# Windowed attention in 256-token units on 64-wide TensorE tiles, issued in a planned order, with the first 128 tokens of the dense expert taken as the stationary operand

## The chip, the cores and the metric

The kernel runs on one core of a Trainium2 chip. The metric is the device time of one execution in microseconds. Before the change it is 609.06 us, the median of three runs (608.77 to 610.55).

Engine names are those of the profile: PE is TensorE, PEld its weight loads, DVE is VectorE, ACT ScalarE, POOL GpSimd, and SP the engine whose queue issues the DMAs.

## The reference

Three layers follow one another, on 1152 tokens (2 sequences of 576) of width 512:

```python
def _attn_ref(q, k, v):                      # (2, 8, 576, 64) each
    scores = scale * np.matmul(q, k.transpose(0, 1, 3, 2))
    mask = (rel >= 0) & (rel < 64)           # rel = query position - key position
    scores = np.where(mask, scores, -1000000000.0)
    attn = softmax(scores)                   # with + 1e-09 in the denominator
    return np.matmul(attn, v)

def _moe_ref(x, domain_probs, w1, w2):       # 4 experts, all of them for every token
    for e in range(E):
        h = np.maximum(x @ w1[e], 0.0)       # 512 -> 1024
        out += p[:, e:e + 1] * (h @ w2[e])   # 1024 -> 512

def _moe2_ref(x, modality_id, w_gate, modality_bias, w1, w2):
    # 8 experts; each token goes through the one that its gate picks
```

## The kernel before, in words

Everything is kept in fp32 precision. The dense products split each operand into a high and a low part of a faster format (xh and xl, wh and wl, hh and hl) and add three products, high x high, high x low and low x high. The attention products run on plain fp32 operands, each of which the chip executes as two passes of a matmul.

**Attention.** A query block of 64 tokens sees its own 64 keys and the 64 before. The kernel works in units of two or three blocks (`units`), one pair of heads at a time: 7 units x 4 head pairs = 28 steps. A step n goes through stages, each a small function: `at_T` transposes q and k (PE), `at_Q` copies k out (ACT) and writes q into a block-diagonal tile `qbd`, so that one 128x128 matmul serves both heads (DVE), `at_K` brings the last 64 keys of the unit before (POOL), `at_S` multiplies to scores on PE, adds the mask and takes the row maxima (DVE), `at_E` takes the exponential with its row sums (ACT), `at_N` makes reciprocals (DVE) and scales (POOL), `at_X` transposes the weights (PE, copy on ACT), `at_O` multiplies by v (PE) and copies the high part (ACT), `at_L` writes the low part xl (DVE). `attn_half` issues one half step, in a software pipeline of five steps: each call holds stages of several steps.

**Expert 0.** Its tokens are taken in groups of 256, 256, 256 and 384. `moe1_group` does the first product in eight parts f of 12 matmuls (`mm1_at`, L346), with the weights stationary and the tokens moving, and then the second product, one 128-token tile at a time, in four parts of six matmuls (`mm2_part`, L372), and `add_x2` writes the result into acc (L382). After each part a hook runs; `hook_e0` lets it issue a quota of attention half steps, so that attention stands between the dense matmuls. Before the first group, 13 attention steps are issued with dummy matmuls (`warm`, L82) between them, and the first three parts f of the first group are fed one slice at a time (`early`).

**Order.** Every engine takes its instructions in the order in which the program issues them. Before, that order is the order of the calls. Behind expert 0 the experts 1 to 3, the gate and the eight routed experts follow; the change does not touch them.

Of the kernel before, what the change touches and what calls it, by code (L numbers as in the profile page):

```python
# [5 lines left out]
F32 = mybir.dt.float32  # L6
# [9 lines left out]
def build(tc, q, k, v, probs, w1, w2, mid, wg, mbias, m2w1, m2w2, out):  # L16
    nc = tc.nc
# [7 lines left out]
    U = 192  # L25
    NU = NT // U
    UPB = S // U
# [3 lines left out]
    with ctx:  # L31
# [10 lines left out]
        pa = ctx.enter_context(tc.tile_pool(name="pa", bufs=1, space=PSUM))  # L42

        ident = const.tile([128, 128], F32, name="ident")
        mask0 = const.tile([128, 3, 128], F32, name="mask0")
        mask1 = const.tile([128, 3, 128], F32, name="mask1")
# [6 lines left out]
        qbd = [const.tile([128, 3, 128], F32, name=f"qbd{i}") for i in range(3)]  # L53

        with tc.manual_schedule():
# [4 lines left out]
            for t in qbd:  # L60
                nc.vector.memset(t, 0.0)

            nc.vector.memset(ident4, 0.0)
            for i in range(4):
                nc.gpsimd.affine_select(out=ident4, in_=ident4, compare_op=ALU.not_equal, fill=1.0,
                                        base=-32 * i, pattern=[[-1, 32]], channel_multiplier=1)
            nc.gpsimd.memset(mask1, 0.0)
            for hh in range(2):
                m = mask1[hh * 64:(hh + 1) * 64]

                nc.gpsimd.affine_select(out=m, in_=m, compare_op=ALU.is_ge, fill=-1.0e9,
                                        base=-1, pattern=[[0, 3], [1, 128]], channel_multiplier=-1)
                nc.gpsimd.affine_select(out=m, in_=m, compare_op=ALU.is_ge, fill=-1.0e9,
                                        base=64, pattern=[[0, 3], [-1, 128]], channel_multiplier=1)
            nc.gpsimd.tensor_copy(out=mask0, in_=mask1)
            nc.gpsimd.memset(mask0[:, 0, 0:64], -1.0e9)

            def warm(n):

                ps = pm.tile([128, 512], F32, tag="mm", name="psW")  # L80
                for _ in range(n):
                    nc.tensor.matmul(out=ps[:, 0:128], lhsT=ident, rhs=ident, start=True, stop=True)  # L82

            qu, ku, vu = {}, {}, {}
# [5 lines left out]
            def load_unit(u, heads=((0, H),)):  # L90
                b, t, nb = units[u]
                if u not in qu:
                    for dst, nm in ((qu, "qu"), (ku, "ku")):
                        dst[u] = at.tile([96, 2, H, D], F32, tag=nm, name=nm)
                n = 32 * nb
                for h0, h1 in heads:
                    for src, dst in ((q, qu), (k, ku)):
                        for r in range(2):
                            nc.sync.dma_start(
                                out=dst[u][0:n, r, h0:h1, :],  # L100
                                in_=src[b, h0:h1, 64 * t:64 * (t + nb), :].rearrange("h (p r) d -> r p h d", r=2)[r])

            def load_v(i):
                b, j = divmod(i, S // 64)
                x = at.tile([128, H * D], F32, tag="vu", name="vu", bufs=6)
                if j == 0:
                    nc.gpsimd.memset(x[0:64], 0.0)
                    nc.sync.dma_start(out=x[64:128].rearrange("p (h d) -> p h d", d=D),
                                      in_=v[b, :, 0:64, :].rearrange("h p d -> p h d"))
                else:  # L110
                    nc.sync.dma_start(out=x.rearrange("p (h d) -> p h d", d=D),
                                      in_=v[b, :, 64 * j - 64:64 * j + 64, :].rearrange("h p d -> p h d"))
                vu[i] = x
# [25 lines left out]
            def load_half(c, half):  # L139
                o = slice(512 * half, 512 * (half + 1))  # L140
                nc.sync.dma_start(out=raw[0, c][:, o], in_=w1[0, 128 * c:128 * (c + 1), o])

# [20 lines left out]
            def split_hi(c, half):  # L163
                key = 0
                if half == 0:
                    wh[c] = wp.tile([128, 1024], F32R, tag=f"wh{c}", name=f"wh{c}")
                    wl[c] = wp.tile([128, 1024], F32R, tag=f"wl{c}", name=f"wl{c}")
                o = slice(512 * half, 512 * (half + 1))
                nc.scalar.activation(out=wh[c][:, o], in_=raw[key, c][:, o], func=ACTF.Copy)

            def split_lo(c, half):
                o = slice(512 * half, 512 * (half + 1))
                eng = nc.gpsimd if c == 2 or (half == 1 and c == 0) else nc.vector
                eng.tensor_tensor(out=wl[c][:, o], in0=raw[0, c][:, o], in1=wh[c][:, o].bitcast(F32), op=ALU.subtract)  # L174
                if half == 1:
                    raw.pop((0, c))
                    cnt["split"] += 1
                    pump()
# [8 lines left out]
            kT = {}  # L187
            kprev = {}
            Tps, Pn, PT, Ops = {}, {}, {}, {}
# [5 lines left out]

            def at_T(n):
                b, t, nb, u, hp = unit_of(n)
                m = 32 * nb
                ps = pa.tile([128, 512], F32, tag="T", name="psT")
                for src, o in ((qu[u], 0), (ku[u], 192)):  # L200
                    for r in range(2):
                        nc.tensor.transpose(out=ps[:, o + m * r:o + m * r + m],
                                            in_=src[0:m, r, 2 * hp:2 * hp + 2, :].rearrange("p h d -> p (h d)"),
                                            identity=ident[0:m, 0:m])
                Tps[n] = ps

            def at_Q(n):
                b, t, nb, u, hp = unit_of(n)
                m = 32 * nb
                ps = Tps.pop(n)  # L210
                kt = kT[n]
                nc.scalar.activation(out=kt[:, 64:64 + 2 * m].rearrange("q (m r) -> q m r", r=2),
                                     in_=ps[:, 192:192 + 2 * m].rearrange("q (r m) -> q m r", r=2), func=ACTF.Copy)
                qb = qbd[n % 3]
                for hh in range(2):
                    nc.vector.tensor_scalar(
                        out=qb[64 * hh:64 * hh + 64, 0:nb, 64 * hh:64 * hh + 64].rearrange(
                            "q i (p r) -> q i p r", r=2),
                        in0=ps[64 * hh:64 * hh + 64, 0:2 * m].rearrange("q (r i p) -> q i p r", r=2, i=nb),
                        scalar1=0.125, scalar2=None, op0=ALU.mult)  # L220

            def at_K(n):

                b, t, nb, u, hp = unit_of(n)
                kt = at.tile([128, 256], F32, tag="kT", name="kT", bufs=5)
                if t == 0:
                    nc.gpsimd.memset(kt[:, 0:64], 0.0)
                else:
                    kp, o = kprev[hp]
                    nc.gpsimd.tensor_copy(out=kt[:, 0:64], in_=kp[:, o:o + 64])  # L230
                kT[n] = kt
                kprev[hp] = (kt, 64 * nb)

            def at_S(n):
                b, t, nb, u, hp = unit_of(n)
                ps = pa.tile([128, 3, 128], F32, tag="S", name="psS")
                kt = kT.pop(n)
# [3 lines left out]
                p = at.tile([128, 3, 128], F32, tag="sm", name="sm", bufs=3)  # L241
                nc.vector.tensor_tensor(out=p[:, 0:nb], in0=ps[:, 0:nb], in1=(mask0 if t == 0 else mask1)[:, 0:nb],
                                        op=ALU.add)
                st = at.tile([128, 8], F32, tag="st", name="st", bufs=3)
                nc.vector.tensor_reduce(out=st[:, 0:nb], in_=p[:, 0:nb], axis=AX.X, op=ALU.max, negate=True)
                stat[n] = (st, p)

            def at_E(n):
                b, t, nb, u, hp = unit_of(n)
                st, p = stat[n]  # L250
                for i in range(nb):
                    nc.scalar.activation(out=p[:, i, :], in_=p[:, i, :], func=ACTF.Exp, bias=st[:, i:i + 1],  # L252
                                         accum_out=st[:, 3 + i:4 + i])
# [851 lines left out]
```

## Time and profile before

| what | before |
|---|---|
| median of 3 runs | 609.06 us (608.77 to 610.55) |
| the profiled execution's own time | 610.33 us |
| its span, first to last instruction | 608.5 us |
| PE busy | 594.0 us, 98% of the span |
| DVE busy | 268.1 us, 44% |
| ACT busy | 205.8 us, 34% |
| POOL busy | 80.8 us, 13% |

An engine's busy time counts its instructions, and matmuls overlap: a row's duration is from its start to its modelled end, while the next one has started. The time that a stream of matmuls takes is read from one start to the next. The x behind a PE row counts passes, so an fp32 matmul of the attention counts twice.

### The profile page before, as it was taken

What the parts mean: (1) busy time and instruction counts of PE and PEld (TensorE: products, weight loads), DVE (VectorE), ACT (ScalarE), POOL (GpSimd) and SP (SyncE); (2) the same over time, 40 slices, a digit from 0 to 9 for tenths busy, and PEclk for the clock granted to TensorE, in tenths of its full rate; (3) what the DMA queues carried; (4) which work ended last, traced back from release to release, by engine and by line L of the source; (5) the groups of instructions that cost most, each with busy time, mean ns of one, the idle gap of its engine ahead of it and who ended that gap; (6) DMA issues with size and microseconds to landing.
All of it is one profiled execution on the core that took longest, in us unless ns stands there. A gap on an engine that the chain in (4) does not pass through costs nothing. (4 is left out here: it accounts for less than half of the span.)

```text
span 608.5 us, 9147 instructions
## 1 busy us (share of the span) xinstructions
PE 594.0 (98%) x3518; PEld 535.8 (88%) x3518; DVE 268.1 (44%) x618; ACT 205.8 (34%) x498; POOL 80.8 (13%) x124
## 2 busy tenths in 40 slices
PE   7989999999999999999999999999999999999995
PEld 6878899999999898989898999989898989897964
DVE  3888866542444121244321242426158598233310
ACT  2788565442313020223110131303043464333420
POOL 3354311111000000000000000000001203324221
PEclk7999999999999999999999999999999999999998
DMA  5776912000134000042200022000403466426520
GB/s 130 195 168 210 236 36 52 3 1 1 68 73 127 12 1 1 0 139 69 71 1 0 1 70 69 1 0 32 160 1 139 123 226 216 155 67 217 170 87 32
DMA packets 56463, 51.10 MB, mean 84 GB/s; under 512 B 41183, under 2 KB 41183, under 8 KB 56416
## 3 DMA queue, kind: packets, MB, share of 16 engines
q1 hardware_dynamic: 54736, 45.19, 25.2%
q0 software_dynamic: 1680, 5.29, 2.5%
q8 instruction: 29, 0.48, 0.3%
q14 instruction: 18, 0.15, 0.1%
HBM read 45.71 MB, written 4.95 MB: 83 GB/s over the span
## 5 line engine op out<-in xcount | busy, mean ns | idle before, releaser
L346 PE MATMUL ps<-xh,wh 128*128 128x384 f32 (+2 forms) x544 | 176.7, 325 | 0.2 <-DVE hl L356 0.2
L346 PE MATMUL ps<-xh,wl 128*128 128x384 f32 (+2 forms) x544 | 173.3, 318 | 1.3 <-DVE wl L174 0.9
L346 PE MATMUL ps<-xl,wh 128*128 128x384 f32 (+2 forms) x544 | 173.4, 319 | 0.0
L355 ACT ACTIVATE hh<-ps 128x384 fp32r<-128x384 f32 (+2 forms) x136 | 61.9, 455 | 288.2 <-PE ps L346 283.5
L372 PE MATMUL ps<-wh,hh 128*128 128x512 f32 (+1 forms) x368 | 146.8, 399 | 0.4 <-DVE hl L356 0.4
L372 PE MATMUL ps<-wh,hl 128*128 128x512 f32 (+1 forms) x368 | 143.8, 391 | 0.0
L372 PE MATMUL ps<-wl,hh 128*128 128x512 f32 (+1 forms) x368 | 143.6, 390 | 0.0
L356 DVE SCALAR_TENSOR_TENSOR hl<-ps,hh 128x384 fp32r<-128x384 f32 (+2 forms) x136 | 69.5, 513 | 138.6 <-ACT hh L355 138.5
L346 PEld LDWEIGHTS ps<-xh,wl 128*128 128x128 f32 x544 | 102.6, 189 | 1.7 <-DVE wl L174 1.1
L346 PEld LDWEIGHTS ps<-xh,wh 128*128 128x128 f32 x544 | 102.5, 188 | 1.2 <-DVE hl L356 0.4
L346 PEld LDWEIGHTS ps<-xl,wh 128*128 128x128 f32 x544 | 102.7, 189 | 0.6
L372 PEld LDWEIGHTS ps<-wh,hh 128*128 128x128 f32 (+1 forms) x368 | 68.8, 187 | 16.0 <-issue 1.7
L372 PEld LDWEIGHTS ps<-wh,hl 128*128 128x128 f32 (+1 forms) x368 | 68.7, 187 | 15.2
L372 PEld LDWEIGHTS ps<-wl,hh 128*128 128x128 f32 (+1 forms) x368 | 68.8, 187 | 13.2
L384 DVE SCALAR_TENSOR_TENSOR acc<-ps,prob,acc 128x512 f32<-128x512 f32 x27 | 20.3, 750 | 94.6 <-PE ps L372 94.6
L160 DVE TENSOR_TENSOR wl<-raw,wh 128x1024 fp32r<-128x1024 f32 x44 | 54.8, 1259 | 9.3 <-ACT wh L156 9.3
L838 POOL DMA_INDIRECT xr<-x2d,idg x11 | 12.4, 1130 | 332.1 <-DVE ids L549 329.5
L156 ACT ACTIVATE wh<-raw 128x1024 fp32r<-128x1024 f32 x52 | 53.3, 1051 | 0.0
L262 POOL TENSOR_TENSOR sm<-sm,rs 128x384 f32<-128x384 f32 (+1 forms) x28 | 21.7, 774 | 90.6 <-DVE rs L261 72.1
L252 ACT ACTIVATE sm<-sm,st 128x128 f32<-128x128 f32 x72 | 27.9, 391 | 0.2
L160 POOL TENSOR_TENSOR wl<-raw,wh 128x1024 fp32r<-128x1024 f32 x8 | 19.3, 2413 | 33.3 <-ACT wh L156 33.2
L287 ACT ACTIVATE xh<-psO 64x192 fp32r<-64x192 f32 (+1 forms) x56 | 16.9, 301 | 19.6 <-PE psO L281 18.3
(176 smaller groups left out, 431.7 us busy)
## 6 DMA issues: line engine op xcount, KB each, us to landing
raw<-in_moe_w_dram SPq DMA_DIRECT2D x56, 512.0 KB, 3.9
vu<-in_v_dram SPq DMA_DIRECT2D x16, 256.0 KB, 3.9
x2d<-acc SPq DMA_DIRECT2D x3, 780.0 KB, 3.5
raw<-in_moe_w_dram SPq DMA_DIRECT2D x8, 256.0 KB, 4.6
acc<-in_moe_w_dram SPq DMA_DIRECT2D x4, 512.0 KB, 7.7
qu<-in_q_dram SPq DMA_DIRECT2D x8, 192.0 KB, 3.4
ku<-in_k_dram SPq DMA_DIRECT2D x8, 192.0 KB, 4.0
qu<-in_q_dram SPq DMA_DIRECT2D x4, 128.0 KB, 3.4
```

The costliest lines, as they stand in the source:

```text
L156: nc.scalar.activation(out=hi, in_=x, func=ACTF.Copy)
L160: eng.tensor_tensor(out=lo[:, o], in0=x[:, o], in1=hi[:, o].bitcast(F32), op=ALU.subtract)
L252: nc.scalar.activation(out=p[:, i, :], in_=p[:, i, :], func=ACTF.Exp, bias=st[:, i:i + 1], accum_out=st[:, 3 + i:4 + i])
L262: nc.gpsimd.tensor_tensor(out=p[:, 0:nb], in0=p[:, 0:nb], in1=rs[:, 0:nb].to_broadcast([128, nb, 128]), op=ALU.mult)
L287: nc.scalar.activation(out=oh, in_=ps[a, 0:nb, a], func=ACTF.Copy)
L346: nc.tensor.matmul(out=ps[:, 0:n], lhsT=a[kk][:, fs], rhs=b_[:, kk, gs], start=(kk == 0 and term == 0), stop=(kk == KD - 1 and term == 2))
L355: nc.scalar.activation(out=hi[:, 0:n], in_=ps[:, 0:n], func=ACTF.Relu)
L356: nc.vector.scalar_tensor_tensor(out=lo[:, 0:n], in0=ps[:, 0:n], scalar=0.0, in1=hi[:, 0:n].bitcast(F32), op0=ALU.max, op1=ALU.subtract)
L372: nc.tensor.matmul(out=ps[0:m], lhsT=a[f][:, ts_], rhs=b_[c][:, o:o + 512], start=(f == 0 and a is hh_t and b_ is wh), stop=(f == KF - 1 a ...
L384: nc.vector.scalar_tensor_tensor(out=o, in0=ps, scalar=prob[:, t, e:e + 1], in1=o, op0=ALU.mult, op1=ALU.add)
L838: nc.gpsimd.indirect_dma_start(out=x, out_offset=None, in_=x2d[0:last, :], in_offset=bass.IndirectOffsetOnAxis(ap=idg[i][:, a:a + 1], axis=0))
```

## The change

**Units.** Attention works on five units of 128, 256, 256, 256 and 256 tokens that run over the border of the two sequences (20 steps: 4 of two blocks, 16 of four). Transposes are 128x128. The block-diagonal tile is gone. `at_S` issues per block and head one matmul with 64 rows (the head's dimension) and 64 result partitions (the block's queries); the two heads of a block write different PSUM banks, and the two blocks of a pair different halves of the partitions. `at_O` issues per block and head one matmul with 64 result partitions and 64 columns. Scale and mask are one DVE instruction (`at_M`); the row sums are a DVE reduction, and the accumulating read on ACT is gone. V is loaded once in 128-token tiles, `va`, and POOL puts the halves of neighbours into `vb`.

**First 128 tokens.** For them the first product of expert 0 is done with the activations stationary and the weights moving, 512 columns at a time (`g0_mm`), then relu, eight transposes (`g0_turn`) and the split. The other groups of expert 0 are four of 256 tokens; the first of them shares its second product with the 128.

**Order.** A list of operations with their engine, an assumed cost and what they need is handed to `in_order`, which repeatedly takes the operation that can start first on its engine; the program is then issued by assumed start. Dummy matmuls are put where PE has an assumed gap before the first 256-token group.

```diff
-            units = [(0, 0, 2), (0, 2, 2), (0, 4, 3), (0, 7, 2), (1, 0, 3), (1, 3, 3), (1, 6, 3)]
+            units = [(0, 2), (2, 4), (6, 4), (10, 4), (14, 4)]
...
             def at_S(n):
...
-                for i in range(nb):
-                    nc.tensor.matmul(out=ps[:, i, :], lhsT=qbd[n % 3][:, i, :], rhs=kt[:, 64 * i:64 * i + 128],
-                                     start=True, stop=True)
+                ps = pa.tile([128, 2, 512], F32, tag="S", name="psS")
...
+                for i in range(nb):
+                    j, i2 = divmod(i, 2)
+                    lo, hi, st = (0, 2, 1) if u == 0 else WIN[i]
+                    for h in range(2):
+                        a = slice(64 * h, 64 * h + 64)
+                        nc.tensor.matmul(out=ps[64 * i2:64 * i2 + 64, h, 128 * j:128 * j + 128],
+                                         lhsT=x[a, 64 * i:64 * i + 64], rhs=kt[a, lo:hi:st],
+                                         start=True, stop=True)
...
+            def at_M(n):
...
+                for h in range(2):
+                    nc.vector.scalar_tensor_tensor(out=p[:, h], in0=ps[:, h, 0:128 * nj].rearrange("p (j c) -> p j c", j=nj),
+                                                   scalar=0.125, in1=m, op0=ALU.mult, op1=ALU.add)
...
             def at_O(n):
...
+                    w = va[t + i - 1] if i2 else vb[t + i] if t + i else va[0]
+                    for h in range(2):
+                        nc.tensor.matmul(out=ps[64 * h:64 * h + 64, 64 * i:64 * i + 64],
+                                         lhsT=w[:, 64 * (2 * hp + h):64 * (2 * hp + h) + 64],
+                                         rhs=pt[:, h, j, 64 * i2:64 * i2 + 64], start=True, stop=True)
...
+            def g0_mm(kk, half):
...
+                o = slice(512 * half, 512 * half + 512)
+                for i, (a, b_) in enumerate(((xh, wh), (xl, wh), (xh, wl))):
+                    nc.tensor.matmul(out=psG[half], lhsT=a[:, kk, 0:G0], rhs=b_[kk][:, o],
+                                     start=(kk == 0 and i == 0), stop=(kk == KD - 1 and i == 2))
...
+            def in_order():
...
+                while left:
+                    best = None
+                    for key, (eng, cost, fn, deps, late, pr) in left.items():
...
+                        if all(d in done for d in deps):
+                            r = max([done[d] + (0.0 if plan[d][0] == eng else late + 0.12) for d in deps], default=0.0)
+                            s = max(r, free.get(eng, 0.0))
+                            if best is None or (s, -chain(key)) < best[0]:
+                                best = ((s, -chain(key)), key)
...
+                return sorted(order, key=lambda x: x[0])
...
+                    dep = [bank(("m1", g, f), ("hl", g, f)), last]
+                    dep += [("L", 4 * g + 7)] + [("lo", c) for c in range(4)]
...
+                    op(last, "PE", 1.44, L(g_mm1, g, f), dep, rank=MM)
...
+            STAGES = dict(K=("POOL", .24, .24, at_K), T=("PE", .24, .47, at_T), Q=("ACT", .4, .6, at_Q),
...
+                if eng == "PE":
+                    if s <= warm_end and s - end > .4 and end > 1:
+                        warm(int((s - end - .1) / .23))
...
-            moe1_group(0, 768, 384, hook_e0((0, 15, False, True)))
...
+            pump()
+            moe1_group(0, G0 + 3 * G1, G1, hook_e0)
```

Three places show what moves on the engines. The first is PE from the start of the program. psW is the dummy matmul, psT the transposes, psS the scores. Before:

```order
L82 MATMUL psW<-ident 128x128 x8
L202 MATMUL psT<-ident,qu 128x64 x2
L202 MATMUL psT<-ident,ku 128x64 x2
L82 MATMUL psW<-ident 128x128 x2
L202 MATMUL psT<-ident,qu 128x64 x2
L202 MATMUL psT<-ident,ku 128x64 x2
L82 MATMUL psW<-ident 128x128 x2
L239 MATMUL psS<-kT,qbd_90 128x128 x2
```

And now:

```order
L78 MATMUL psW<-ident 128x128 x12
L209 MATMUL psT<-ident,acc 128x128 x2
L78 MATMUL psW<-ident 128x128 x2
L209 MATMUL psT<-ident,acc 128x128 x2
L241 MATMUL psS<-qk 64x128 x4
```

Twelve dummy matmuls now stand ahead of the first transposes, where eight did, and the scores of the first step follow the second step's transposes. (q and k of the early units lie in memory that later becomes acc.)

The second place is PE in the first 256-token group of expert 0. psG is the product with the activations stationary, ps the ordinary first product, psO the product with v, psX the transposed weights. Before, the fourth part of the first group:

```order
L346 MATMUL ps_689<-xh,wl_599 128x256
L239 MATMUL psS<-kT,qbd_92 128x128 x3
L202 MATMUL psT<-ident,qu 128x64 x2
L202 MATMUL psT<-ident,ku 128x64 x2
L281 MATMUL psO<-pt,vu 128x128 x3
L271 MATMUL psX<-ident,sm 128x128 x3
L346 MATMUL ps_754<-xh,wh_452 128x256
```

And now, where the first 256-token group begins:

```order
L488 MATMUL psG<-wl_521,xh 128x512
L209 MATMUL psT<-ident,ku 128x2x64
L209 MATMUL psT<-ident,qu 128x128
L209 MATMUL psT<-ident,ku 128x2x64
L209 MATMUL psT<-ident,qu 128x128
L312 MATMUL psO<-pt,vb 64x64 x2
L312 MATMUL psO<-pt,va 64x64 x2
L312 MATMUL psO<-pt,vb 64x64 x2
L312 MATMUL psO<-pt,va 64x64 x2
L78 MATMUL psW<-ident 128x128 x2
```

The product with v is four pairs of 64-wide matmuls for a step of four blocks, where it was one 128x128 matmul per block. Behind these rows stand the transposes of one more step, the scores of the ninth step and then 48 dense matmuls in a row. By then the steps 0 to 7 have been issued whole.

The third place is PE at the last border of expert 0, where attention ends. Now:

```order
L363 MATMUL ps_1765<-wh_677,hl 128x512
L312 MATMUL psO<-pt,vb 64x64 x2
L312 MATMUL psO<-pt,va 64x64 x2
L312 MATMUL psO<-pt,vb 64x64 x2
L312 MATMUL psO<-pt,va 64x64 x2
L293 MATMUL psX<-ident,sm 128x128 x4
L312 MATMUL psO<-pt,vb 64x64 x2
L312 MATMUL psO<-pt,va 64x64 x2
L312 MATMUL psO<-pt,vb 64x64 x2
L312 MATMUL psO<-pt,va 64x64 x2
L335 MATMUL ps_1907<-xh,wh_211 128x256
```

The last two products with v and the last transposes stand directly ahead of the last dense group, with no second-product matmuls between them. Before, the last attention step stood inside the third group's second product.

## Rows read from the trace of the kernel before

**Rows 1.** The page, busy us of each engine.

```profile
PE 594.0 (98%) x3518; PEld 535.8 (88%) x3518; DVE 268.1 (44%) x618; ACT 205.8 (34%) x498; POOL 80.8 (13%) x124
```

**Rows 2.** Stages: from:to, us; PE, PEld, DVE, ACT, POOL busy; PEclk, DMA share, GB/s.

```profile
10.00:20.00 10.00, 10.00 (x56) 8.79 (x56) 6.09 (x20) 4.28 (x18) 1.58 (x4) 0.60 0.89 214
20.00:42.74 22.74, 19.50 (x158) 17.20 (x156) 20.28 (x65) 19.51 (x77) 9.35 (x17) 1.00 0.72 181
42.74:175.88 133.14, 131.48 (x884) 121.69 (x885) 75.17 (x191) 63.84 (x210) 26.13 (x53) 1.00 0.29 79
175.88:608.50 432.62, 426.10 (x2395) 382.22 (x2393) 164.26 (x335) 116.37 (x193) 38.10 (x28) 1.00 0.24 77
```

**Rows 3.** Timeline of PE at one attention step: start, us, operation, passes.

```profile
79.29 0.83 PE L239 MATMUL psS<-kT,qbd 128*128 128x128 f32 x6
...
80.23 0.37 PE L346 MATMUL ps<-xh,wh 128*128 128x256 f32 x1
80.44 0.28 PE L346 MATMUL ps<-xl,wh 128*128 128x256 f32 x1
80.56 0.28 PE L346 MATMUL ps<-xh,wl 128*128 128x256 f32 x1
...
81.74 0.83 PE L281 MATMUL psO<-pt,vu 128*128 128x128 f32 x6
82.41 0.49 PE L271 MATMUL psX<-ident,sm 128*128 128x128 f32 x3
82.65 0.37 PE L346 MATMUL ps<-xh,wh 128*128 128x256 f32 x1
```

**Rows 4.** Timeline of DVE, the last two writes of expert 0 into acc.

```profile
170.50 0.75 DVE L382 TENSOR_SCALAR acc<-ps,prob 128x512 f32<-128x512 f32 x1 [2.42 <-PE ps L372]
...
175.94 0.75 DVE L382 TENSOR_SCALAR acc<-ps,prob 128x512 f32<-128x512 f32 x1 [4.69 <-PE ps L372]
```

**Rows 5.** Timeline of PE at the few-token product on 32-column tiles (128*32).

```profile
578.25 0.32 PE L346 MATMUL ps<-xl,wh 128*128 128x352 f32 x1
578.41 0.32 PE L346 MATMUL ps<-xh,wl 128*128 128x352 f32 x1
578.65 1.92 PE L960 MATMUL psF<-acc,xg 128*32 128x512 f32 x16
580.51 0.50 PE L372 MATMUL ps<-wh,hh 128*128 128x512 f32 x1
```

**Rows 6.** Timeline of PE in the start-up.

```profile
1.37 3.48 PE L82 MATMUL psW<-ident 128*128 128x128 f32 x16 [1.37 <-POOL ident L58]
4.78 0.33 PE L202 MATMUL psT<-ident,qu 64*128 64x64 f32 x2
...
15.12 1.06 PE L239 MATMUL psS<-kT,qbd 128*128 128x128 f32 x4
...
18.06 0.61 PE L239 MATMUL psS<-kT,qbd 128*128 128x128 f32 x4
...
32.34 0.44 PE L271 MATMUL psX<-ident,sm 128*128 128x128 f32 x2 [0.93 <-POOL sm L262]
```

**Rows 7.** DVE and ACT by line and shape, 0 to 176 us: busy, mean ns.

```profile
L356 DVE SCALAR_TENSOR_TENSOR hl<-ps,hh 128x256 fp32r<-128x256 f32 x24 | 10.2, 424 | 14.8 <-ACT hh L355 14.7
L245 DVE TENSOR_REDUCE st<-sm 128x3 f32<-128x384 f32 x16 | 8.8, 553 | 0.6
L160 DVE TENSOR_TENSOR wl<-raw,wh 128x1024 fp32r<-128x1024 f32 x6 | 7.5, 1272 | 0.7 <-ACT wh L156 0.7
L298 DVE TENSOR_TENSOR xl<-psO,xh 64x128 fp32r<-64x128 f32 x24 | 6.9, 288 | 1.6 <-ACT xh L287 1.1
L245 DVE TENSOR_REDUCE st<-sm 128x2 f32<-128x256 f32 x12 | 5.0, 420 | 0.4
L261 DVE RECIPROCAL rs<-st 128x3 f32<-128x3 f32 x16 | 2.8, 176 | 0.5
...
L355 ACT ACTIVATE hh<-ps 128x256 fp32r<-128x256 f32 x24 | 9.0, 377 | 16.8 <-PE ps L346 16.6
L273 ACT ACTIVATE pt<-psX 128x384 f32<-128x384 f32 x16 | 7.9, 491 | 0.6 <-PE psX L271 0.2
```

More of the change, by code (lines that the diff above doesn't have):

```diff
@@ L103, in load_v @@
[L103 to L113, printed above, removed]
+            qu, ku, va, vb = {}, {}, {}, {}
@@ L222, in at_K @@
[L222 to L232, printed above, removed]
+                for j in range(nb // 2):
+                    for src, o in ((ku[u], 64 * nb), (qu[u], 0)):
+                        dst = ps[:, o + 128 * j:o + 128 * j + 128]
+                        if nb == 4 and o:
+                            dst = ps[:, o:o + 256].rearrange("p (o a c) -> p a o c", o=2, a=2)[:, j]
+                        nc.tensor.transpose(out=dst, in_=src[:, j, 2 * hp:2 * hp + 2, :].rearrange("p h d -> p (h d)"),
+                                            identity=ident)
@@ L280, in at_O @@
                 for i in range(nb):
[L281 to L287 removed]
+                    j, i2 = divmod(i, 2)
@@ new lines, in in_order, with chain @@
+            def in_order():
+                users = {k: [] for k in plan}
+                for k, v_ in plan.items():
+                    for d in v_[3]:
+                        users[d].append(k)
+                tail = {}
+                def chain(k):
+                    if k not in tail:
+                        eng, cost, _, _, late, (r, _) = plan[k]
+                        tail[k] = cost * (1.3 if r == MM else 1.0) + late + .12 + max([chain(x) for x in users[k]], default=0.0)
+                    return tail[k]
+                free, done, left, order = {"SP": .75}, {}, dict(plan), []
+                while left:
+                    best = None
+                    for key, (eng, cost, fn, deps, late, pr) in left.items():
+                        if eng == "SP" and any(left[k][0] == "SP" and left[k][5][1] < pr[1] for k in left):
+                            continue
+                        if all(d in done for d in deps):
[3 more added lines that the diff above has]
+                                best = ((s, -chain(key)), key)
+                    (s, _), key = best
+                    eng, cost, fn, deps, late, pr = left.pop(key)
+                    free[eng] = s + cost
+                    done[key] = s + cost + (2.8 if eng == "SP" else 0.0)
+                    order.append((s, s + cost, eng, key, fn))
+                return sorted(order, key=lambda x: x[0])
@@ new lines, in build, with hook_e0 @@
+            at_ctx.close()
+            pa_ctx.close()
+            pa = ctx.enter_context(tc.tile_pool(name="pa", bufs=1, space=PSUM))
+            def hook_e0(kind, idx, part):
+                if kind == "2" and idx < 2 and part in (0, 2):
+                    split_next()
+            nc.vector.memset(ident4, 0.0)
+            for i in range(4):
+                nc.gpsimd.affine_select(out=ident4, in_=ident4, compare_op=ALU.not_equal, fill=1.0,
+                                        base=-32 * i, pattern=[[-1, 32]], channel_multiplier=1)
```

526 lines of the change are left out of this document (303 added, 223 removed).

## The prediction

> **What bounds the kernel now.** I read the page's busy times first: TensorE (PE) is busy 594.0 of 608.5 us, more than twice any other engine [rows 1]. So work on PE, or time in which PE cannot start, is all that counts. Second, the span cut in stages [rows 2]: from 175.88 us on runs what the change leaves alone, 432.62 us of it. That border is the last write of expert 0 into acc, which starts at 175.94 us [rows 4]. From 42.74 to 175.88 us PE does expert 0 with the attention steps pushed between its matmuls, and idles 133.14 − 131.48 = 1.7 us: that stage is a plain sum of PE work. Before 42.74 us PE has attention, dummy matmuls and only 48 dense ones; there VectorE (DVE) is busy 20.28 of 22.74 us, so the chain of attention through DVE sets when dense work can begin. I forecast the new place of the border, E, and carry the 432.62 us over. The profiled execution took 610.33 us, 1.83 around its span and 1.27 above the median 609.06; I subtract that 1.27 at the end.
>
> **Dense work, part by part.** A token tile of the second product (24 matmuls 128x512) takes 175.94 − 170.50 = 5.44 us [rows 4]; there are nine before and after: 49.0 us. Twelve 128x256 matmuls of the first product take 1.42 us: 80.23 to 81.74 us is 1.51, in which the first after attention costs 0.21 where the next costs 0.12 [rows 3]. After, there are 32 such groups: 45.4 us. The eight groups of 384 columns go, and in their place stand 24 matmuls 128x512 for the first 128 tokens with the activations stationary. The columns streamed are equal (96 x 384 = 96 x 256 + 24 x 512), so this edit alone is worth nothing on PE but eight transposes, 0.08 us each by the three in 0.24 us [rows 3]. What it buys is that those 24 need one 128-token unit of attention, and stand in the start-up; after it, 49.0 + 45.4 + 0.9 for the transposes and the switch = 95.3 us of dense work remain.
>
> **Attention on PE.** Before, a step of three 64-token blocks takes 79.29 to 80.23 us for S and T and 81.74 to 82.65 us for O and X, plus 0.09 twice for the return to dense work: 2.0 us [rows 3]. S and O run as two passes per matmul, 0.11 us each (six of O in 0.67 us). After, a step of four blocks has the same eight 128-column transposes as four T and four X (0.08 each, 0.33 and 0.33 us), and S and O become eight matmuls, 16 passes each, on tiles of 64 rows or columns. No row of before has a 64-wide tile. The nearest is the few-token matmul on 32-column tiles [rows 5]: 16 passes of 512 columns, four tiles. It holds PE from 578.57 (0.16 after the start of the last dense matmul, by the 0.16 between it and the one before) to 580.51: 1.94 us. Passes of 128 columns take 0.11 us, so 16 of 512 in a row would take about 7.0 us, and four side by side 1.71. They do run side by side, with 0.23 us for entering and leaving. S has the same four tiles and 128 columns: 4 x 0.11 + 0.23 = 0.67 us. O has two tiles and 64 columns: 8 rounds between 0.055 us (half of 0.11, if the columns set the pace) and 0.11 (if something else does) + 0.23, 0.67 to 1.11; I take 0.80, nearer to the row that scales with columns. With 0.09 for two returns, a step is 0.33 + 0.33 + 0.67 + 0.80 + 0.18 = 2.3 us. From below a step cannot cost less than 1.7 (no price of switching, O at 0.44). From above, tiles one after the other: 16 x 0.11 + 0.23 = 2.0 each for S and O, 4.8 us a step. I take 2.3, because the row shows four tiles at once.
>
> The Trainium skill, "TensorEngine Tiling (Array Packing)", Key Properties, speaks against the change here: changing the tiling mode drains the engine, and this kernel would now do so twice for each S and O among dense matmuls. The trace agrees that a change costs something, and the 0.23 us of rows 5 is that price; it is in the sum 24 times in the dense stage.
>
> At the first dense group of 256 eight of the 20 steps are done, and T of two more and S of one are issued (order shown above): 12 x 2.3 − 2 x 0.33 − 0.67 = 26.3 us of attention remain.
>
> **Where the dense groups start.** The last write of xl for tokens 128 to 383 must be done. DVE carries the chain. The first step needs 24 dummy passes first, where before had 16 from 1.37 to 4.78 us, 0.21 us each [rows 6]; the eight more cost 0.11 to 0.21 us each, so T stands at about 6.1 us instead of 4.8. T (0.33), the copy on ScalarE (ACT, 0.38), S of two blocks (0.45) and three hand-overs of 0.1 put DVE's first mask at 7.6 us. DVE work of a two-block step [rows 7]: two masks at 0.29, two reductions of 256 at 0.42, two small ones at 0.17, one xl at 0.29 and seven gaps of 0.04: 2.33 us, four times 9.3. A four-block step: two masks at 0.42, two reductions of 512 (0.42 and 0.55 for 256 and 384 give 0.69), 0.34, xl 0.42, 0.28: 3.27, four times 13.1. Three weight splits at 1.27 and the relu of 128x512 (0.75 as in rows 4) stand among them: 4.6. In all 27.0 us. At DVE's share of 0.89 from rows 2 all the way, the end is 7.6 + 30.3 = 37.9 us; with the 0.61 of 10 to 20 us it does 7.6 us by 20 us and needs 19.4 / 0.89 = 21.8 more, 41.8 us. I take the middle, 39.8, since both stretches are this chain's. Data is not late: the 4.25 MB needed by then are there at about 25 us at the 214 GB/s of rows 2. The other loads, which the new order puts behind them on SP's queue (expert 1's first weights behind the last V tile), fall where the DMA engines are 0.29 busy and are wanted tens of us later. Beside DVE's chain, at no cost, lie ACT, which loses an accumulator read per softmax block but was busy 19.51 of the 22.74 us and would be late next, and POOL, which takes the new copies of V and of keys and was busy 9.35 [rows 2]; if POOL's copies held up O, each would cost some 0.5 us at the start and nothing later.
>
> **What PE waits for later.** The order puts the next unit's T and S between the last O of a unit and its dense group, so about 0.5 us at two borders. At the last border nothing is left: X, its copy on ACT (0.49 at 384, 0.6 at 512), O, the copy out (0.38), xl (0.42) and four hand-overs: 1.9 us beside PE's own part [rows 7]. With 1.7 us of chance waits as before: 4.6 us. The softmax of the last step is covered by three second-product pieces and four attention pieces on PE (7 us against 5.6).
>
> **Sum.** E = 39.8 + 95.3 + 26.3 + 4.6 = 166.0 us, 9.9 before the old 175.9. 610.33 − 9.9 − 1.27 = **599.2 us**. The tails of the unknowns for this case alone: start 37 to 44, step 2.0 to 2.7, waits 3 to 8: 593 to 606.
>
> **Rivals.**
>
> *Better than the sum* (0.14): the start at 37, O at 0.67 and S at 0.55 (a step of 2.06), waits of 3 us: E = 37 + 95.3 + 23.5 + 3 = 158.8, so 592.0. For it, DVE at 0.89 already from 20 us; against, 0.61 in the ten before.
>
> *The start slips* (0.10). From 10 to 20 us the granted clock was 0.60 [rows 2], S took 1.06 us and later 0.61 for the same four passes [rows 6]: PE ran at the 1.2 GHz level while its work was thin and came back to 2.4 after a stretch without idling. Some 30 dummy matmuls are planned into gaps; at the low level they take 0.43 instead of 0.22 us and fill 6.3 us more, and with 2 us for the attention pieces themselves, most of which DVE's chain hides, the start comes at 48.1: 607.5, no change. The Trainium skill, "TensorE: Matmul & The Clock Gate", Part 4, says that transposes do not count towards the full clock as matmuls do; no run here separates that, and by it this rival would gain weight at the same price.
>
> *Tiles not side by side* (0.08). Row tiles, which S uses beside column tiles, are not in the trace. Passes in a row at half the weights' width, 0.055, give S 1.11 and O 1.11: 12 x 0.75 = 9 us more, 608.2; at the full 0.11, 12 x 2.5 = 30 us more, 629.
>
> *Waits in PE's order* (0.12), the slower side: PE takes the planned order as it comes. Twelve steps put 48 attention pieces into it, each behind a chain through ACT, DVE and POOL, with one PSUM buffer each. If each waits 0.45 us, 21.6 us are lost, 1.7 of them already in the sum: 619.1. It decides from (9.9 + 1.7) / 48 = 0.24 us a piece. For it: before, X waited up to 0.93 us on POOL in the start-up [rows 6]; against: one dense piece of 1.4 us stands between most of them.
>
> **How the numbers follow.** Forecast 0.56, the rest as given. What a measurement can tell from no change is 0.3%, 1.8 us: faster means under 607.2. Faster: 0.56 less a tail of 0.02, 0.14, 0.04 of the slipping start and 0.02 of the tiles: 0.74. Same: 0.09, from the forecast's tail, the slipping start and tiles at half price. Slower 0.17. The range 589 to 614 leaves out half of the serial tiles, most of the waits and the best end of the better case.
>
> **What would show it.** In the profile after, the last acc write of expert 0 stands at 166 (159 to 176); the first 128x256 dense matmul at 40; S of a four-block step holds PE 0.6 to 0.8 us, O 0.7 to 1.1; waits on PE between these two marks sum to 3 to 8 us; the stage behind the border again takes 432 to 433 us. If that last differs, the premise is wrong; if S or O takes over 1.5 us, or the first dense matmul starts after 46 us, the sum is.

## The result, and the profile after

The changed kernel takes 599.42 us (median of 4 runs, 599.19 to 599.78) beside 609.64 us of the kernel before: a ratio of 0.9833, with a 95% interval of 0.9815 to 0.9851. The prediction was 599.2 us. The profiled execution took 599.78 us. One of the four runs of one kernel below, the third low half on DVE, took 1170.8 us, and its ratio leaves that run out. PE is still what bounds the kernel; this is the page's line on busy times, answering [rows 1]:

```profile
PE 585.7 (98%) x3830; PEld 517.9 (87%) x3830; DVE 250.5 (42%) x537; ACT 192.1 (32%) x379; POOL 92.5 (15%) x139
```

The stages, with the columns of [rows 2]; the first 128x256 dense matmul starts at 38.88 us, and expert 0 ends at 164.73:

```profile
10.00:20.00 10.00, 9.00 (x106) 6.72 (x106) 8.25 (x27) 8.25 (x21) 6.35 (x14) 1.00 1.15 295
20.00:38.88 18.88, 17.96 (x211) 14.21 (x209) 13.29 (x29) 14.15 (x33) 17.20 (x23) 1.00 0.84 195
38.88:164.73 125.85, 124.15 (x1070) 107.30 (x1067) 63.09 (x143) 49.74 (x128) 27.21 (x59) 1.00 0.21 54
164.73:598.00 433.27, 426.06 (x2394) 382.05 (x2392) 164.25 (x335) 116.46 (x193) 38.16 (x28) 1.00 0.23 78
```

In the last row PE's work is that of before, 426.06 us. In the second the busy column to look at is the fifth: POOL works 17.20 of 18.88 us, where it worked 9.35 of 22.74 (some of it already for the dense stage), and DVE fell from 20.28 to 13.29. DVE's last two writes of expert 0 into acc, answering [rows 4]:

```profile
159.29 0.75 DVE L373 TENSOR_SCALAR acc<-ps,prob 128x512 f32<-128x512 f32 x1 [1.72 <-PE ps L363]
164.73 0.75 DVE L373 TENSOR_SCALAR acc<-ps,prob 128x512 f32<-128x512 f32 x1 [2.42 <-PE ps L363]
```

The border moved from 175.94 to 164.73, 11.2 us. PE's timeline at X and O, and at T, O, T and S, of the dense stage (start, us, tile size, passes), answering [rows 3]:

```profile
70.87 0.60 PE L293 MATMUL psX<-ident,sm 128*128 128x128 f32 x4
71.39 0.34 PE L312 MATMUL psO<-pt,vb 128*64 128x64 f32 x4
...
72.01 0.50 PE L363 MATMUL ps<-wh,hh 128*128 128x512 f32 x1
72.35 0.40 PE L363 MATMUL ps<-wl,hh 128*128 128x512 f32 x1
72.58 0.39 PE L363 MATMUL ps<-wh,hl 128*128 128x512 f32 x1
...
76.14 0.60 PE L209 MATMUL psT<-ident,acc 128*128 128x128 f32 x4
76.67 0.34 PE L312 MATMUL psO<-pt,vb 128*64 128x64 f32 x4
...
78.01 0.67 PE L241 MATMUL psS<-qk 64*64 64x128 f32 x16
78.61 0.39 PE L335 MATMUL ps<-xh,wh 128*128 128x256 f32 x1
```

From one start to the next: X 0.52, O 0.62, T 0.53, S 0.60. The first dense matmul after O holds PE 0.34, the next 0.23: the return costs 0.11. All that PE waits for from 38.88 to 164.73 us (us in total, times, longest):

```profile
PE ps L335 <- DVE hl L512: 0.8, 1, 0.8
PE psO L312 <- ACT pt L301: 0.7, 1, 0.7
```

The changed kernel again, on the chip of three later runs: 600.1 us, ratio 0.9843 (0.9826 to 0.9861), border 165.25. A difference of half a microsecond between profiles is therefore nothing. It is there from the start: DVE's first mask, here and in the repeat,

```profile
8.00 0.49 DVE L253 SCALAR_TENSOR_TENSOR sm<-psS,mk 128x128 f32<-128x128 f32 x2 [8.00 <-PE psS L241]
8.50 0.49 DVE L253 SCALAR_TENSOR_TENSOR sm<-psS,mk 128x128 f32<-128x128 f32 x2 [8.50 <-PE psS L241]
```

and from there to the border it is 156.73 and 156.75 us. In the profiles below the first mask lies between 7.24 and 8.73 us, so two borders are best compared from it. Why it moves in kernels whose beginning is the same stays open.

> The changed kernel unaltered, on the same chip as the three others: 599.4, border 164.7.

### The profile page after: what moved, and what is told of

It reads as the page before. It is cut to its first block, busy times and chain, and to the rows that moved or that the text cites. A ratio compares the mean times of both kernels' runs of the same rounds, so it can differ in the third digit from the quotient of the medians.

```text
span 598.0 us, 9432 instructions
## 1 busy us (share of the span) xinstructions
PE 585.7 (98%) x3830; PEld 517.9 (87%) x3830; DVE 250.5 (42%) x537; ACT 192.1 (32%) x379; POOL 92.5 (15%) x139
## 3 DMA queue, kind: packets, MB, share of 16 engines
HBM read 43.61 MB, written 4.95 MB: 81 GB/s over the span
## 5 line engine op out<-in xcount | busy, mean ns | idle before, releaser
L335 PE MATMUL ps<-xh,wh 128*128 128x384 f32 (+2 forms) x544 | 173.8, 320 | 0.8 <-DVE hl L512 0.8
L335 PE MATMUL ps<-xh,wl 128*128 128x384 f32 (+2 forms) x544 | 171.1, 315 | 0.0
L347 ACT ACTIVATE hh<-ps 128x384 fp32r<-128x384 f32 (+2 forms) x112 | 52.1, 465 | 259.2 <-PE ps L335 254.6
L348 DVE SCALAR_TENSOR_TENSOR hl<-ps,hh 128x384 fp32r<-128x384 f32 (+2 forms) x112 | 58.1, 522 | 118.1 <-ACT hh L347 118.1
L167 DVE TENSOR_TENSOR wl<-raw,wh 128x1024 fp32r<-128x1024 f32 x42 | 52.0, 1253 | 9.2 <-ACT wh L163 9.2
L163 ACT ACTIVATE wh<-raw 128x1024 fp32r<-128x1024 f32 x48 | 49.1, 1052 | 0.0
L284 POOL TENSOR_TENSOR sm<-sm,rs 128x512 f32<-128x512 f32 (+1 forms) x20 | 21.0, 1051 | 40.0 <-DVE rs L277 38.8
L267 ACT ACTIVATE sm<-sm,st 128x128 f32<-128x128 f32 x72 | 23.2, 392 | 5.8 <-DVE st L256 5.8
L253 DVE SCALAR_TENSOR_TENSOR sm<-psS,mk 128x256 f32<-128x256 f32 (+1 forms) x40 | 14.0, 391 | 23.1 <-PE psS L241 23.1
L1042 POOL DMA_INDIRECT out_dram<-y,ids x11 | 11.3, 1025 | 57.4 <-ACT y L1040 32.6
```

The costliest lines, as they stand in the source:

```text
L163: nc.scalar.activation(out=hi, in_=x, func=ACTF.Copy)
L167: eng.tensor_tensor(out=lo[:, o], in0=x[:, o], in1=hi[:, o].bitcast(F32), op=ALU.subtract)
L253: nc.vector.scalar_tensor_tensor(out=p[:, h], in0=ps[:, h, 0:128 * nj].rearrange("p (j c) -> p j c", j=nj), scalar=0.125, in1=m, op0=ALU.m ...
L267: nc.scalar.activation(out=p[:, h, j], in_=p[:, h, j], func=ACTF.Exp, bias=st[:, o:o + 1])
L284: nc.gpsimd.tensor_tensor(out=p, in0=p, in1=rs.rearrange("p (h j) o -> p h j o", h=2).to_broadcast([128, 2, nj, 128]), op=ALU.mult)
L335: nc.tensor.matmul(out=ps[:, 0:n], lhsT=a[kk][:, fs], rhs=b_[:, kk, gs], start=(kk == 0 and term == 0) if first is None else (first and te ...
```

## The experiments

Each varies the changed kernel.

### Are 64-wide tiles side by side, and what does S cost?

Tile by tile: all matmuls of one tile ahead of the next one's.

```diff
-                for i in range(nb):
+                for h in range(2):          # at_S; i then runs over 0, 2, 1, 3
+                    for i in [2 * j + i2 for i2 in range(2) for j in range(nb // 2)]:
...
-                for i in range(nb):
+                for h in range(2):          # at_O
+                    for i in range(nb):
```

> Same matmuls as the changed kernel, but S and O issue all passes of one 64-wide tile before the next tile's (S: per tile 4 passes in a row, O: 8), so that neighbours in the order share a tile. Theory 'side by side' (the price of S and O comes from tiles that work at the same time): S of a four-block step goes from 0.60 us to about 1.5 (13 of 16 passes of 128 columns no longer overlap, 0.107 us each), O from 0.62 to about 1.0 (16 passes of 64 columns at 0.055); 12 steps in the dense stage and 8 in the start-up, so the border of expert 0 moves from 164.7 to about 181 us and the time to about 614. Rival 'narrow is cheap by itself' (passes were never overlapped, each is just short): no change, 599 within 1 us.

603.38 us, ratio 0.9917 (0.9890 to 0.9944); border 168.30. The theory's 614 us and S of 1.5 us did not come. PE's timeline at O, and at S:

```profile
36.72 0.33 PE L311 MATMUL psO<-pt,vb 128*64 128x64 f32 x2
...
37.62 0.71 PE L78 MATMUL psW<-ident 128*128 128x128 f32 x4
...
38.69 0.69 PE L240 MATMUL psS<-qk 64*64 64x128 f32 x16
39.31 0.39 PE L334 MATMUL ps<-xh,wh 128*128 128x256 f32 x1
```

O grew from 0.62 to 0.90, S stayed at 0.62. Over the stage O took 10.8 us in place of 7.7: this and a start 0.4 later are the 3.6 us by which the border moved. The rival, that passes never overlap and order means nothing, is out for O: its two tiles run side by side, and lose that by order. On S this run decides nothing. Two more ask S itself, in the eleven steps 9 to 19: all its matmuls twice, or each with 256 columns of keys in place of 128 (the two edits are shortened).

```diff
-                    for h in range(2):
+                    for h in (0, 1, 0, 1):                       # S twice
```

> S of the eleven steps 9 to 19 issues its eight matmuls twice, with the same operands and the same result; nothing else differs from the changed kernel (599.4). Theory, PE's work adds up one for one in the dense stage: S holds PE 0.60 us there, some 0.2 of it for the change of tiles, so the second eight cost about 0.4 each time, 11 x 0.4 = 4.4 us: 603.8, with the border at 169. Rival, part of S lies in time in which PE would have waited or filled its queue anyway: under 2 us in all, 600 to 601.

```diff
-  out=ps[64 * i2:64 * i2 + 64, h, 128 * j:128 * j + 128], rhs=kt[a, lo:hi:st]
+  out=ps[64 * i2:64 * i2 + 64, h, 128 * j:128 * j + 256], rhs=kt[a, 0:4]     # S wide
```

> In the eleven steps 9 to 19 each of the eight matmuls of S streams 256 columns of the keys in place of 128 (the softmax reads the same tile, with other numbers in it); the number of matmuls and passes stays. Doubling the passes cost 0.49 us a step. Theory, columns on tiles side by side set S's pace: the wider S costs the same 0.49 us more, 11 x 0.49 = 5.4: 605 and the border at 170. Rival, the number of passes (each with weights of its own to load) sets it: under 0.15 us a step, under 1.7 in all: 599.5 to 601.

Twice: 605.18 us, 0.9933 (0.9916 to 0.9950), border 169.67. Wide (other scores): 604.56 us, 0.9913 (0.9888 to 0.9938), border 170.15 from a start at 39.58. PE's timeline, S twice:

```profile
65.31 1.16 PE L242 MATMUL psS<-qk 64*64 64x128 f32 x32
66.40 0.50 PE L364 MATMUL ps<-wh,hh 128*128 128x512 f32 x1
```

and S wide:

```profile
66.39 1.09 PE L242 MATMUL psS<-qk 64*64 64x256 f32 x16
67.42 0.50 PE L364 MATMUL ps<-wh,hh 128*128 128x512 f32 x1
```

1.09 and 1.03 us in place of 0.60: sixteen more passes cost 0.49, sixteen times 128 more columns 0.43. In a row, sixteen passes at the 0.11 of [rows 3] would be 1.76: four run at once, columns set the pace, and 0.11 to 0.17 us of the 0.60 belong to neither. The stage grew by 5.43 us with S twice (131.28 for 125.85), 11 x 0.49, and by 4.72 with S wide, 11 x 0.43; counted from the first mask it began at 30.88 us in all three kernels. What PE does here adds up one for one, as the prediction's sum took it. The rival "S costs nothing extra" is out.

### What carries the start-up?

Three edits. The 24 matmuls of the first 128 tokens wait until the start-up's attention is done:

```diff
-  [("L", hp), ("lo", hp), ...]
+  [("L", hp), ("L", 7), ("S", 8), ("lo", hp), ...]
```

> The 24 matmuls of the first 128 tokens wait for the last L of unit 1 and S of step 8, so they stand behind the start-up instead of inside it; nothing else is changed, and the planner puts dummy matmuls where they were. Theory 'the start-up is not PE's' (PE had spare time there, so the 24 matmuls were free): their 6.3 us by the trace are added, border 164.7 to 170 or 171, time about 605.5. Rival 'the start-up's end is PE's own work' (PE is the bound from 32 us on, and the matmuls only change place): the dense groups start as much earlier as the matmuls come later, border within 1.5 us of 164.7, time 599 to 601.

603.84 us, 0.9930 (0.9905 to 0.9955), border 169.01. The 24 matmuls and the returns to them hold PE 6.3 us of the start-up; moved out, they put the border 4.3 us later, 4.7 from the first mask. The last O of the start-up comes no earlier without them (36.94 us, in the changed kernel 36.59). So most of their 6 us was hidden: up to that O, PE's work did not bound the start-up.

The low half of the third weight, four pieces on POOL, goes to DVE:

```diff
-                e_ = (nc.vector, nc.gpsimd, nc.gpsimd, nc.vector)[c]
+                e_ = (nc.vector, nc.gpsimd, nc.vector, nc.vector)[c]
```

> The low part of weight chunk 2 is made by DVE in one piece (1.2 us) instead of by POOL in four (2.9 us). Theory of the prediction, 'DVE carries the start-up': DVE has 1.2 us more before the last L of unit 1, the border goes from 164.7 to about 166, time about 600.8. Rival 'POOL carries it' (in the profile after POOL is busy 17.2 of the 18.9 us before the first dense group, DVE 13.3): POOL has 2.9 us less, border about 162 to 163, time 597 to 598.

597.93 us, 0.9826 (0.9784 to 0.9867); once more on another chip 598.32, 0.9818 (0.9798 to 0.9837). First dense matmul at 37.68 and 37.66 (38.88 and 39.39 in the changed kernel), border 163.43 and 163.42 (164.73 and 165.25): from the first mask 1.4 us earlier in both pairs, though the ratios alone do not part the two kernels. With more work on DVE the start-up became shorter, so DVE's load does not carry it. Work taken off POOL shortens it. POOL in the changed kernel:

```profile
26.12 2.11 POOL L177 TENSOR_TENSOR wl<-raw,wh 128x256 fp32r<-128x256 f32 x3
28.19 1.04 POOL L284 TENSOR_TENSOR sm<-sm,rs 128x512 f32<-128x512 f32 x1
29.19 0.73 POOL L177 TENSOR_TENSOR wl<-raw,wh 128x256 fp32r<-128x256 f32 x1
29.87 2.04 POOL L284 TENSOR_TENSOR sm<-sm,rs 128x512 f32<-128x512 f32 x1
31.87 0.72 POOL L177 TENSOR_TENSOR wl<-raw,wh 128x256 fp32r<-128x256 f32 x1
```

Not a gap: the softmax scaling (L284), for which X waits, alternates with pieces of weights (L177); the third weight's last piece ends at 32.6 us. With that weight on DVE:

```profile
27.95 1.87 POOL L284 TENSOR_TENSOR sm<-sm,rs 128x512 f32<-128x512 f32 x1 [0.18 <-DVE rs L277]
30.40 1.90 POOL L284 TENSOR_TENSOR sm<-sm,rs 128x512 f32<-128x512 f32 x1 [0.59 <-DVE rs L277]
```

POOL now waits for DVE's reciprocals, and its last scaling ends later, not earlier: at 32.30 us, before at 31.91. So the scalings are not the way. Two other things moved. The third weight's low half is ready at 28.9 us, and nine more of the 24 matmuls of the first 128 tokens stand ahead of the start-up's last X. The changed kernel has dummies and a wait there instead, 1.4 us between 29.43 and 31.96, and those matmuls behind them. PE in the changed kernel:

```profile
30.80 0.71 PE L78 MATMUL psW<-ident 128*128 128x128 f32 x4
31.96 0.66 PE L293 MATMUL psX<-ident,sm 128*128 128x128 f32 x4 [0.46 <-POOL sm L284]
32.38 0.48 PE L488 MATMUL psG<-wh,xh 128*128 128x512 f32 x1
```

and with the third low half on DVE:

```profile
29.52 0.39 PE L488 MATMUL psG<-wh,xh 128*128 128x512 f32 x1
...
33.53 0.66 PE L293 MATMUL psX<-ident,sm 128*128 128x128 f32 x4
```

And the new plan lets DVE write xl of step 6 at 34.06 us, ahead of a weight of the second product; it stood behind one, at 35.74. The start-up's last O starts at 35.25 in place of 36.59. Which of the two did it, no run separates.

The first dense matmul is not the same mark in both kernels: S of step 8 and T of step 9, 1.1 us of PE, stand ahead of it in the changed kernel and behind it here, and 1.8 us of dummies stand ahead of it here. That the border gains 1.4 us all the same is owed to the dense stage, where attention costs 0.5 us more for those two pieces and the waits are 0.5 us less.

> The kernel with the third low half on VectorE once more, on the same chip as the one without the last dummies: 597.9, border 163.4, first dense matmul at 37.7.

Third, only the first eight of the planner's dummy matmuls stay:

```diff
-                        warm(int((s - end - .1) / .23))
+                        pass
```

> The eight dummy matmuls at the very start stay, the 37 others go (4 of them directly behind the first eight). Theory 'the clock needs them': the granted clock falls to its 1.2 GHz level in parts of 5 to 36 us, PE pieces there take twice as long, and the border comes 2 to 5 us later: time 601 to 605. Rival 'they only delay': the first T comes 1.3 us earlier, nothing else slows, the border comes 0.5 to 1.5 us earlier: time 598 to 599.

600.11 us, 0.9866 (0.9834 to 0.9898), border 164.99. Its stage from 10 to 20 us, and what PE waited for most before 39 us (1.4 in the changed kernel):

```profile
10.00:20.00 10.00, 8.48 (x73) 6.03 (x74) 7.06 (x23) 7.22 (x18) 5.07 (x11) 0.66 0.97 262
```

```profile
PE psX L293 <- POOL sm L284: 4.4, 5, 1.4
```

The granted clock fell to 0.66 in that stage, from 1.00. The first dense matmul came at 39.11, 0.23 later, although the first transposes came 1.2 us earlier (4.95, for 6.18) and the first mask 0.8 (7.24): from the first mask the border is 1.0 us later. Neither expectation held as put: the clock does fall, and the loss is about a microsecond, most of it made up by the earlier beginning.

### Does the start's gain last?

Besides the third low half on DVE, the high halves of the second product's four weight pieces wait on ACT until the start-up is over:

```diff
-                op(("hi", c), "ACT", 1.05, L(split_hi, c), [("w", c), ("C", 7)])
+                op(("hi", c), "ACT", 1.05, L(split_hi, c), [("w", c), ("L", 7)])
```

> The third weight's low half is split on VectorE in place of GpSimd, as in the run before, and the high halves of the second product's four weight pieces wait on ScalarE until the eighth attention step has left xl, so that they don't stand in the start-up. Theory (GpSimd carried the start-up, and with that gone ScalarE is one of two next): first dense matmul at about 37.0, border at 162.5, 597.0. Rival (VectorE is next, or PE, which had no idle time after 32.4 us): no different from the kernel with the third low half alone, 597.9.

598.94 us, 0.9827 (0.9813 to 0.9842). The first dense matmul starts at 37.57, but the border is at 164.54: what it won at the start it lost behind it, and from the first mask (8.47) it is 0.7 us later than with the low half alone. The theory is out; by the ratios the rival, no difference, holds. The waits on PE in the dense stage:

```profile
PE psHT L503 <- DVE hl L512: 1.2, 1, 1.2
PE psO L312 <- ACT pt L301: 0.7, 1, 0.7
PE ps L335 <- DVE hl L512: 0.6, 1, 0.6
```

2.5 us, for 1.1 with the low half alone on DVE: a new wait at the transposes of the first tokens' activations, behind the low halves (hl) of the group's first product, which now come late on DVE.

And the third low half on DVE without the last eight dummy matmuls (35.87 to 37.68 us):

```diff
-                    if s <= warm_end and s - end > .4 and end > 1:
+                    if s <= 25 and s - end > .4 and end > 1:
```

> The third weight's low half on VectorE as before, and the eight dummy matmuls ahead of the first 128x256 dense matmul left out (they stood from 35.87 to 37.68 us there). Theory (with GpSimd relieved, the start ends with the last unit's O, a copy of 0.38, xl of 0.42 and three hand-overs of 0.1 behind 35.9, so at 37.0, and the dummies hold it up by 0.7): first dense matmul at 37.0, border at 162.8, 597.3. Rival (xl is later than that, or the order behind it changes): no different from the same kernel with the dummies, or slower, 598 and above.

597.34 us, 0.9801 (0.9780 to 0.9822), the lowest of all, though its interval overlaps that of the kernel with the dummies on the same chip (0.9798 to 0.9837). PE's timeline at the first dense group:

```profile
36.51 0.38 PE L335 MATMUL ps<-xh,wh 128*128 128x256 f32 x1
...
37.73 0.39 PE L335 MATMUL ps<-xh,wh 128*128 128x256 f32 x1
38.19 0.39 PE L335 MATMUL ps<-xl,wh 128*128 128x256 f32 x1
```

The first dense matmul comes 1.15 us earlier, the border 0.29 (163.13). But the first mask came 0.67 later in this profile (8.73, for 8.06): from it, the first dense matmul is 1.8 us earlier and the border 1.0, as much as the medians differ. Nine matmuls use the first three head pairs; the tenth is the first on xh of the fourth, and the eleventh, which needs its xl, comes 0.46 us behind it. So the dummies did hold the start-up up, and without them that xl ends it, at about 38 us.

### Do pieces in PE's order wait?

The planner is told that every stage on ACT, DVE and POOL lasts half as long, so it puts their followers on PE earlier.

```diff
-  op((s_, n), eng, c2 if nb == 2 else c4, ...)
+  op((s_, n), eng, (c2 if nb == 2 else c4) * (1.0 if eng == "PE" else .5), ...)
```

> Only the planner's numbers change: it is told that every step of attention on ScalarE, VectorE and GpSimd lasts half as long as in the changed kernel, so it puts the dependent pieces on PE earlier among the dense matmuls. Rival of the prediction (waits in PE's order are what this kernel is at risk of): each of the 48 attention pieces of the dense stage waits some 0.25 us, 12 us in all: 611. Theory (one dense piece of 1.4 us between pieces hides most of it): waits on PE between the first dense matmul and the border grow from 1.6 to some 3 to 6 us, and the time to 601 to 604.

609.25 us, 1.0006 (0.9993 to 1.0018): the whole gain is gone. Waits on PE from the first dense matmul to the border, and that stage in the columns of [rows 2]:

```profile
PE psO L312 <- ACT pt L301: 5.6, 4, 1.8
PE ps L335 <- DVE hl L512: 1.6, 1, 1.6
PE psT L209 <- ACT qk L222: 1.6, 2, 0.8
PE psS L241 <- DVE sm L253: 1.2, 2, 0.7
```

```profile
39.54:174.39 134.85, 124.78 (x1089) 107.20 (x1088) 61.86 (x146) 53.19 (x131) 29.01 (x59) 1.00 0.20 52
```

PE's busy time is the changed kernel's within 0.6 us; 10.0 us are waits, in nine places, up to 1.8 us each. The theory expected 3 to 6 and was too low. The rival had the size nearly right, but as a small wait at each of 48 pieces: it is few pieces, each issued 0.5 to 1.8 us before what it needs was ready.

## Why the prediction was right, and where it was not

The place of the border, E, by the prediction's terms; the measured column sums PE's timeline from one start to the next.

| term, us | predicted | measured |
|---|---|---|
| start of the dense groups | 39.8 | 38.9 |
| dense work, with 24 returns from attention (95.3 + 2.2) | 97.5 | 99.2 |
| attention on PE, without returns (26.3 − 2.2) | 24.1 | 24.9 |
| waits in the dense stage | 4.6 | 1.6 |
| border E | 166.0 | 164.7 |
| behind the border | 432.6 | 433.3 |

The measured terms end 0.2 us before the border: there PE has already begun on expert 1.

**The bound** held: PE's work and waits ahead of the border decide, S twice added 11 x 0.49 us and no less. The stage behind the border had the same 426.06 us of PE work; the 0.7 us more is about what the runs here differ by in that unchanged stage, 432.7 to 433.3.

**Attention** held as a sum, of parts that miss in both directions. O took 0.62 and not 0.80: the reading that columns alone set the pace, 0.67, was the better end. S took 0.60, not 0.67, with four tiles at once as rows 5 suggested. X and T took 0.52 to 0.59, not 0.33, where S or O follows, and 0.35 to 0.43 where dense work follows: the way into 64-wide tiles falls on what stands before them, and not on X and T as such. Errors of 0.2 both ways in one step left 0.8 us over twelve steps; that they cancel was luck.

The Trainium skill says in "TensorEngine Tiling (Array Packing)", Key Properties, that a change of the tiling mode drains the engine. The traces agree that a change costs something: 0.11 to 0.17 us of S are neither passes nor columns, and the last dense matmul ahead of S or O holds PE some 0.09 us longer than ahead of T or X (0.32, for 0.23, in the second product). Together that is about the 0.23 of the sum. That it is a drain, no run shows. One reading was wrong: before does have 64-wide tiles, the transposes on 64x128 in [rows 6]; they do not tell whether tiles run side by side.

**Dense work** was 1.7 us short. The returns are 24, as counted, and cost 0.11 in place of 0.09, some 0.5 us in all. What was left out is the way from dense work into S or O, in nine places 0.09 us, 0.8 in all; the rest is spread thin. The nine tiles of the second product, taken at the 5.44 of a stretch without attention [rows 4], 49.0 in all, took 51.6, 17 of the returns included (50.9 in before).

**The start-up** gave the right number by the wrong mechanism. The step "DVE carries the chain" failed. DVE is busy 13.29 of 18.88 us there, and work put onto it shortened the start-up. POOL, which the prediction set down as cover "busy 9.35" at no cost, had got the copies of V and of keys, and its pieces of the third weight, done at 32.6 us, held back matmuls of the first 128 tokens; taken off it, they gave 1.4 us. Whether by those matmuls or by the new order on DVE is open, and so is what bounds the start-up after that. A sum of DVE's work scaled by a busy share of 0.61 to 0.89 could be made to give anything from 37.9 to 41.8; that it held 38.9 shows nothing. The remark that POOL's copies might cost 0.5 us at the start named the engine, though not the work.

**Waits** were 1.6, not 4.6. Two show: for a low half of the first 256-token group, at 44.2 us, where DVE is late (below), and for the weights of the last O, where attention ends, at 141.6 (0.75 of the 1.9 priced there). The rest of what was counted does not show.

**Rivals.** *Waits in PE's order*: real, though as nine waits and not 48; it is held off by the numbers given to the planner, and with half the costs it takes back the 10 us. *Tiles not side by side*: out, by S twice, S wide and O's loss in the other order. *The start slips*: with the planned dummies the granted clock was 1.00 from 10 to 20 us; without them it fell to 0.66, and that run lost 1.0 us from the first mask, not 8. *Better than the sum*: O and S together took the 1.22 us that it gave them, and the waits were lower still; the start, 1.9 us later than there, the transposes and the dense work took the gain back.

## What to carry to other kernels

One engine's work, scaled by a busy share, does not tell when a start-up through five engines ends: add what the change puts on each, the "free" engine first, and ask which pieces wait for it. A busy engine is a suspect, not yet the cause: here its visible waits were not the way by which relieving it helped. Compare two profiles from a mark that has the same work ahead of it in both. An order from assumed costs is worth as much as those costs: costs too low by half undid a gain of 10 us while PE's work stayed the same, so take them from a trace. And when a chain's last link is freed, look at the next one at once: of 1.8 us won at the first dense matmul, 1.0 reached the end.

## What the runs showed of the hardware

**POOL and DVE hold each other up.** The same scaling (L284) takes POOL 1.04 us at 28.19 and 2.04 at 29.87 (rows above). DVE in the changed kernel:

```profile
28.64 0.61 DVE L276 TENSOR_SCALAR st<-st 128x4 f32<-128x4 f32 x1
...
29.78 1.23 DVE L177 TENSOR_TENSOR wl<-raw,wh 128x1024 fp32r<-128x1024 f32 x1
```

and with the third low half on DVE:

```profile
27.72 1.20 DVE L177 TENSOR_TENSOR wl<-raw,wh 128x1024 fp32r<-128x1024 f32 x1
...
29.88 0.17 DVE L276 TENSOR_SCALAR st<-st 128x4 f32<-128x4 f32 x1
30.18 1.22 DVE L177 TENSOR_TENSOR wl<-raw,wh 128x1024 fp32r<-128x1024 f32 x1
```

Each scaling that takes 1.87 to 2.04 us starts while DVE splits a 128x1024 weight (1.2 us), and the 128x4 instruction takes DVE 0.61 us inside a scaling of POOL's and 0.17 where POOL is idle. It goes the other way too, and there it reaches PE. In the changed kernel

```profile
40.34 2.41 POOL L177 TENSOR_TENSOR wl<-raw,wh 128x1024 fp32r<-128x1024 f32 x1
40.48 3.34 DVE L177 TENSOR_TENSOR wl<-raw,wh 128x1024 fp32r<-128x1024 f32 x1
```

DVE's split, begun inside POOL's, takes 3.34 us; the low half behind it comes late, and PE waits 0.8 us for it at 44.2. The Trainium skill says so in "SBUF — State Buffer", Who interferes with whom: a DVE instruction with two SBUF inputs and a GpSimd instruction that reads SBUF contend, and whoever issues first blocks the other. The traces agree for the scalings and the splits; the 128x4 instruction has one SBUF input, which this sentence does not cover. No run was made to take the overlap away.

**S does not mind its order, O does.** Eight matmuls on four 64x64 tiles took 0.60 us alternating and 0.62 tile by tile; eight on two 128x64 tiles 0.62 and 0.90. Why S keeps its overlap is open.
